# Attention's small results in PSUM banks of their own, the first batch's states turned ahead of the rest, and another order of the interleaved steps, in a block-recurrent attention and switch-routing kernel

## The chip, the cores and the metric

The kernel runs on one core of one Trainium2 chip, in one launch. The metric is device time in microseconds. All arithmetic is fp32 apart from a few counting matmuls in bf16.

## The reference

Eight batches, each with 8 heads, 512 tokens `x` and 32 states of width 64. Every token attends to the 32 states of its head and batch, and every state attends to the 512 tokens. The outcome is 8 x (512 + 32) = 4352 rows of 512 numbers, and each row is sent through one of eight experts, the one with the largest gate logit.

```python
scores = scale * np.matmul(x, state.transpose(0, 1, 3, 2))
a = np.exp(scores - scores.max(-1, keepdims=True)); a /= a.sum(-1, keepdims=True) + 1e-09
xread = np.matmul(a, state)
scores2 = scale * np.matmul(state, x.transpose(0, 1, 3, 2))
a2 = np.exp(scores2 - scores2.max(-1, keepdims=True)); a2 /= a2.sum(-1, keepdims=True) + 1e-09
sread = np.matmul(a2, x)
x = concatenate([xread, sread], axis=2).transpose(0, 2, 1, 3).reshape(B * S, H * D)
logits = x @ w_gate;  expert_idx = argmax(logits);  gate_w = softmax(logits)[expert_idx]
for e in range(E):
    xe = x[expert_idx == e]
    out[expert_idx == e] = gate_w * (np.maximum(xe @ w1[e], 0.0) @ w2[e])
```

## The kernel before

A token's row is a mix of the 32 states of its batch, so all 512 tokens of a batch lie close together and are taken to go to one expert, which `guess` works out from the states alone; a repair at the end handles batches where that fails. The matmul with `w1` is then done on the states (`states_w1`, giving `G`), not on the tokens. From batch 1 on, `lists` sorts the 1024 hidden units by a bound: units that are positive for every token (up to 512 of them, `CAPP`) need no relu and are folded into one matrix `M`; units of unknown sign (up to 192) are computed as they are. The kept units' columns of `G` are scattered to a table in DRAM (`g_dram`), loaded back in order (`gp`), and the matching rows of `w2` gathered (`w2c`). Batch 0 runs through `in_full` without that.

**The program's order is written out by hand.** Every engine keeps the order in which the code issues. The main line is `in_full` for batch 0 and `batch(b)` for batches 1 to 7; it calls `insert()` 16 times in batch 0 and 13 times in every later batch. I call these calls slots 0, 1, 2, ... In `batch(b)`: slot 0 follows the transposes `pgu`; slots 1 to 4 come after every second pair of matmuls into `pm`; slots 5 and 6 after the two `phu` groups; slots 7, 8 and 9 inside and after the first pair of `py` banks; slots 10, 11 and 12 inside and after the second. In a slot a plan (L763 and L765) advances generators by one step, one letter each:

- **A**, attention. `back(b)` has four steps: the transposes of `a2` with their copies `a2T`; the state sums `pw` and gate logits `pl`, with the loads of `x` for batch b+2; the norm bound `pq`; the expert count. Beside them run `front(b+1)`'s five: two halves of the transposes of `x`, the scores, the exponentials, the norm.
- **S**, `lists(b)` for a later batch: two steps for `G` (with the load of the next `w1`), four of transposes `pgt` and copies to `gt`, one of marks, one of ranks (`rank`) with eight scatters by GpSimd. The ninth step calls `fetch(b)`: three loads `gp` and six gathers `w2c`, all on GpSimd's queue.
- **M**, `mask(b+1)`, on VectorE.
- **R**, the 256 state rows, which go to experts one by one. When four batches are attended, `sort_states(t)` (five steps) puts 128 of them in groups of 32 by expert and scatters them to `ss_dram`; `rounds` then loads 128 rows (`xg`) and multiplies them by their experts' weights: two halves of `w1` (`pgh`), transposes (`pth`), and `w2` (`pgy`, in two halves of four pieces). There are three rounds, two for t = 0 and one for t = 1. A round takes 16 pieces of 1 MB, each four 256 KB loads on SyncE's queue into a ring of four buffers (`s`); after each group of four pieces is used, `fetch(4)` issues the next four, which wait for the buffers.

PSUM has 8 banks. Four belong to the tile `pa`: its half `pc` holds the scores, the other half (L95, `pa[:, :, 1, :]`) the small results of `guess` and `back`. The other four are handed out in turn by `bank()` (L98) for everything else. Order in the head: the states are loaded in one go (`stn`), all turned (`turn_states(0)`), all batches' experts guessed, the weights of batch 0 requested, then `turn_states(1)` and `front(0)`.

Of the kernel before, what the change touches and what calls it, by code (L numbers as in the profile page):

```python
# [20 lines left out]
def kernel(  # L21
# [39 lines left out]
    DM = H * D  # L61
# [33 lines left out]
    pa = ps_a.tile([128, 4, 2, 256], FP32, name="pa")  # L95
    pc = pa[:, :, 0, :]

    def bank(shape=(128, 512), name="p"):  # L98
# [3 lines left out]
    stn = att.tile([128, 16, D], FP32, tag="a2", name="stn")  # L102
    sp.dma_start(out=stn[:].rearrange("p j d -> p (j d)"),
                 in_=state.rearrange("b h (u j) d -> (b h u) (j d)", u=2))
# [8 lines left out]
    load_x(0, sp)  # L113
    wg = const.tile([128, NDC, E], FP32)
    act.dma_start(out=wg[:], in_=moe_w_gate.rearrange("(c p) e -> p c e", p=128))
    load_x(1, act)
# [32 lines left out]
    blank = att.tile([128, XW], I32, tag="a2T", name="blank")  # L149
# [10 lines left out]
    aTs, stT = {}, const.tile([128, B, H, 2, NS], FP32, name="stT")  # L160
# [9 lines left out]
    srow = const.tile([128, NT, XW], FP32)  # L170
    more = const.tile([128, NT], FP32)


    std = [sst.tile([128, 16, 2, D], FP32, tag="s", bufs=RING, name="std") for _ in range(2)]
    for i in range(2):
        dve.tensor_copy(out=std[0][:, :, i], in_=stn[:])
    for i in range(2):
        act.copy(std[1][:, :, i, 0:32], stn[:, :, 32:64])
        act.copy(std[1][:, :, i, 32:64], stn[:, :, 0:32])
# [10 lines left out]
    def turn_states(v):  # L190
        to = stT[:].rearrange("p b h v (u j) -> p v j (b h) u", u=2)
        for k in range(4):
            pt = pa[:, k].rearrange("p a (j r) -> p (a j) r", j=2) if v == 0 else bank((128, 4, 128), "pst")[:]
            for i in range(4):
                j = 4 * k + i
                pe.transpose(pt[:, i, :], std[v][:, j].rearrange("p i d -> p (i d)"), ident[:])
            evict(to[:, v, ts(k, 4)], pt.rearrange("p j (m u) -> p j m u", u=2))

    def guess():
        for b in range(B):  # L200
            for q in range(4):
                for g in range(2):
                    pe.matmul(pa[ts(q, 32), 2 + g, 1, ts(b, E)], lhsT=stT[ts(g, 64), b, 2 * q + g, 0, :],
                              rhs=wg[ts(g, 64), q, :], start=True, stop=True, skip_group_check=True)
        act.copy(gst[:, :, :, 0:E].rearrange("p b g e -> p g b e"),
                 pa[:, 2:4, 1, 0:B * E].rearrange("p g (b e) -> p g b e", b=B))
        pr = pa[:, 0, 1, 0:B * E].rearrange("p (b e) -> p b e", b=B)
        for g in range(2):
            pe.matmul(pr, lhsT=ones_f[:], rhs=gst[:, :, g, 0:E], start=(g == 0), stop=(g == 1),
                      skip_group_check=True)  # L210
        mx = att.tile([128, B, 1], FP32, name="g_mx")
        dve.tensor_reduce(mx[:, :, 0], pr, AX.X, ALU.max)
        cc = att.tile([128, B, E], FP32, name="g_cc")
        dve.tensor_tensor(cc[:], pr, mx[:].to_broadcast([128, B, E]), ALU.is_ge)
        dve.tensor_tensor(cc[:], cc[:], io8[:].unsqueeze(1).to_broadcast([128, B, E]), ALU.mult)
        dve.tensor_reduce(eb[:], cc[:], AX.X, ALU.max)
        dve.tensor_scalar(e_at[:], eb[:], float(F), None, ALU.mult)
# [19 lines left out]
    def scores(xt, st):  # L237
        for g in range(2):
            for u in range(2):
                for q in range(4):  # L240
                    for i in range(4):
                        pe.matmul(pa[ts(q, 32), i, 0, ts(g, 128)], lhsT=st[ts(i, 32), 2 * q + g, u ^ (i % 2), :],
                                  rhs=xt[ts(i, 32), 2 * q + g, :, u, :],
                                  start=(u == 0), stop=(u == 1), skip_group_check=True)
# [24 lines left out]
    def front(b):  # L269
# [5 lines left out]
        sx = scores(xt, stT[:, b])  # L275
# [16 lines left out]
    def back(b):  # L292
        sx, a2, s2 = soft.pop(b)
        aTs[b] = turn_read(sx)
        if b > 0:
            sq = att.tile([128, 2, S], BF16, tag="sq", name="sq")
            act.activation(sq[:], tokens_of(aTs[b]), AF.Square, bias=off[:, 0:1])
        a2T = att.tile([128, 2, NC, 128], FP32, tag="a2T", name="a2T")
        for g in range(2):
            for c in range(NC):  # L300
                pe.transpose(pa[:, 2 * g + c // 2, 1, ts(c % 2, 128)], a2[:, g, c, :], ident[:])
            act.copy(a2T[:, g].rearrange("p (k c) r -> p k (c r)", k=2), pa[:, ts(g, 2), 1, :])
# [3 lines left out]
        pw = pa[:, 0, 1, 0:128].rearrange("p (g d) -> p g d", g=2)  # L306
# [12 lines left out]
        pl = pa[:, 1, 1, 0:128]  # L319
# [5 lines left out]
        dve.transpose(lg[:].rearrange("p c e -> p (c e)"), pl)  # L325
# [11 lines left out]
        pr = pa[:, 2, 1, 128:128 + E]  # L337
        for c in range(NC):
            pe.matmul(pr, lhsT=ones_b[:], rhs=oh[:, NC * b + c, :], start=(c == 0), stop=(c == NC - 1),
                      skip_group_check=True)  # L340
        dve.tensor_copy(out=cnt[:, b], in_=pr)
# [40 lines left out]
    def states_w1(w1t, st, G, k):  # L382
        pg = [bank(name="pG") for _ in range(2)]
        for q in range(4):
            for g in range(2):
                pe.matmul(pg[g][ts(q, 32), :], lhsT=st[ts(g, 64), 2 * q + g, 0, :],
                          rhs=w1t[ts(g, 64), q, ts(k, 512)], start=True, stop=True, skip_group_check=True)
        for g in range(2):
            evict(G[g][:, ts(k, 512)], pg[g][:])
# [48 lines left out]
    def lists(b):  # L438
# [3 lines left out]
        for k in range(2):  # L442
            states_w1(w1t, stT[:, b], G, k)
# [51 lines left out]
    def fetch(b):  # L495
# [3 lines left out]
        for u in range(2):  # L499
            gp.dma_start(out=t[ts(u, 64), NP + 1], in_=g_dram[b % 2][ds(CAPP + 128, 64)])  # L500
        rows = moe_w2.rearrange("e f d -> (e f) d")
        w2cs[b] = [wpool.tile([128, DM], FP32, tag="w2c", bufs=W2B, name="w2c") for _ in range(NP + NU)]
        for j in range(NP + NU):
            gp.indirect_dma_start(
                out=w2cs[b][j][:], out_offset=None, in_=rows,
                in_offset=bass.IndirectOffsetOnAxis(ap=t[:, j, GW - 1:GW].bitcast(I32), axis=0),
# [14 lines left out]
    def batch(b, insert):  # L521
        t, w2c, a = gps.pop(b), w2cs.pop(b), aTs.pop(b)
# [8 lines left out]
        for g in range(2):  # L531
# [5 lines left out]
            act.copy(M[:, g, :], pm[:])  # L537
        hu = [ffn.tile([128, S], FP32, tag="hu", bufs=NU, name="hu") for _ in range(NU)]
# [25 lines left out]
    def sort_states(t):  # L564
        sp.dma_start(out=srow[:, t, 0:DM], in_=st_dram[ts(t, 128)])
# [4 lines left out]
        for c in range(NDC):  # L570
            pe.transpose(pt[:, c, :], srow[:, t, ts(c, 128)], ident[:])
# [3 lines left out]
        for c in range(NDC):  # L575
# [21 lines left out]
        dve.tensor_copy(out=srow[:, t, DM:DM + 1], in_=gw[:, NX + t])  # L597
        dve.tensor_copy(out=srow[:, t, DM + 1:DM + 2].bitcast(I32), in_=tok_s[:, t:t + 1])
        gp.indirect_dma_start(
            out=ss_dram[t][:], out_offset=bass.IndirectOffsetOnAxis(ap=slot_i[:, 0:1], axis=0),  # L600
            in_=srow[:, t, :].bitcast(I32), in_offset=None, bounds_check=NG * 32 - 1, oob_is_err=False)
# [10 lines left out]
    def rounds(t, r0, r1):  # L612
# [4 lines left out]
        def round_in(r):  # L617
            xgs[r] = sst.tile([128, XW], FP32, tag="xg", bufs=1, name="xg")
            sp.dma_start(out=xgs[r][:].bitcast(I32), in_=ss_dram[t][ts(r, 128)])
# [25 lines left out]
        for r in range(r0, r1):  # L645
# [22 lines left out]
            py = bank(name="pgy")  # L668
            for f in range(NFC):
                four(py, hT[:, ts(f, 128)], r, 2, f, 0, f == 0, f == NFC - 1)  # L670
                if f == 3:
                    fetch(4)
                    yield
            y = ffn.tile([128, DM], FP32, tag="y", bufs=3, name="ys")
            dve.tensor_scalar(y[:], py[:], xg[:, DM:DM + 1], None, ALU.mult)
# [7 lines left out]
    turn_states(0)  # L683
    guess()
    load_w1(0, expert_of(eb, 0))
    w2x = load_w2(expert_of(eb, 0))
    off = const.tile([128, 1], FP32)
    gp.memset(off[:], -1.0 / NS)
    U128 = const.tile([128, 128], BF16)
    dve.tensor_scalar(U128[:], colf[:], iota_p[:, 0:1], None, ALU.is_gt)  # L690
    turn_states(1)
    for _ in front(0):
        pass
# [4 lines left out]
    def late_constants():  # L698
        tmp = const.tile([128, 1], FP32)
# [9 lines left out]
        dve.scalar_tensor_tensor(slot_u[:, 1:2], iota_p[:], 128.0, tmp[:], ALU.add, ALU.add)  # L709

    attended = [0]

    def attention():
        for b in range(B):
            for _ in run(back(b), *([front(b + 1)] if b + 1 < B else [])):
                yield
# [3 lines left out]
    listed = [0]  # L720

    def listing():
        for b in range(1, B):
            for i, _ in enumerate(lists(b)):
                while i == 5 and bounded[0] < b:
                    yield
                yield
            fetch(b)
            listed[0] = b
            yield  # L730

    def masking():
        for b in range(1, B):
            while listed[0] < b:
                next(todo["S"])
# [10 lines left out]
    todo = {"A": attention(), "S": listing(), "R": tokens(), "M": masking()}  # L746
# [12 lines left out]
    for k in range(2):  # L759
        states_w1(w1t, stT[:, 0], G, k)  # L760
    load_w1(1, expert_of(eb, 1))
    late_constants()
    in_full(G, aTs[0], w2x, store_batch(0), inserts("A,A,AS,AS,AS,AS,AS,AS,S,S,S,A,AS,AS,AS,ASM"))  # L763
    for b in range(1, B):
        batch(b, inserts("SA,SA,SA,SA,SA,SR,SR,SR,SR,AR,RA,RA,RM"))  # L765
    for k in "ASMR":
# [30 lines left out]
    with tc.If(number(rest_i[0:1, 0:1], B * E + NT * NG) > 0):  # L797
# [4 lines left out]
        with tc.If(number(n_i[0:1, 0:1], B * E) > 0):  # L802
# [8 lines left out]
            with tc.For_i(0, n_pairs, 1):  # L811
# [23 lines left out]
                st_x = att.tile([128, 1, H, 2, NS], FP32, tag="sq", name="st_x")  # L835
                dve.tensor_copy(out=st_x[:], in_=stT[:, ds(bb, 1)])
# [9 lines left out]
                sx = scores(xt, st_x[:, 0])  # L846
# [21 lines left out]
                for k in range(2):  # L868
                    states_w1(w1s["x"], st_x[:, 0], G, k)
# [32 lines left out]
```

## Time and profile before

| | us |
|---|---|
| four runs: median (lowest to highest) | 571.96 (570.4 to 573.04) |
| the profiled execution | 573.04 |
| its span, first to last instruction | 571.2 |
| busy: TensorE / VectorE / GpSimd / ScalarE | 449.9 / 200.8 / 130.4 / 125.5 |

TensorE's stages, by the first transposes `pgu` of each batch (for batch 0 by its first matmul `pG`):

| stage | from, to (us) | length | TensorE busy | DMA share |
|---|---|---|---|---|
| head | 0 to 37.2 | 37.2 | 15.72 | 0.84 |
| batch 0 | 37.2 to 117.2 | 80.0 | 69.58 | 0.48 |
| batch 1 | 117.2 to 172.7 | 55.5 | 45.23 | 0.39 |
| batch 2 | 172.7 to 235.2 | 62.5 | 44.95 | 0.48 |
| batch 3 | 235.2 to 357.5 | 122.3 | 100.86 | 0.79 |
| batch 4 | 357.5 to 426.6 | 69.1 | 56.34 | 0.57 |
| batch 5 | 426.6 to 469.8 | 43.2 | 30.70 | 0.42 |
| batch 6 | 469.8 to 541.5 | 71.7 | 62.85 | 0.84 |
| batch 7 and the end | 541.5 to 571.2 | 29.7 | 23.62 | 0.15 |

Lines of the timeline give the start, the duration, the engine (PE is TensorE's matmul, PEld its weight load, DVE VectorE, ACT ScalarE, POOL GpSimd, SP SyncE, a q its queue), the operation, output<-inputs and the count; in brackets stand the engine's idle time before it and what ended that. A busy TensorE is not one at its peak: matmuls are pipelined and a matmul that waits inside a group stretches the group.

### The profile page before, as it was taken

What the parts mean: (1) busy time and instruction counts of PE and PEld (TensorE: products, weight loads), DVE (VectorE), ACT (ScalarE), POOL (GpSimd) and SP (SyncE); (2) the same over time, 40 slices, a digit from 0 to 9 for tenths busy, and PEclk for the clock granted to TensorE, in tenths of its full rate; (3) what the DMA queues carried; (4) which work ended last, traced back from release to release, by engine and by line L of the source; (5) the groups of instructions that cost most, each with busy time, mean ns of one, the idle gap of its engine ahead of it and who ended that gap; (6) DMA issues with size and microseconds to landing.
All of it is one profiled execution on the core that took longest, in us unless ns stands there. A gap on an engine that the chain in (4) does not pass through costs nothing. (4 is left out here: it accounts for less than half of the span.)

```text
span 571.2 us, 8799 instructions
## 1 busy us (share of the span) xinstructions
PE 449.9 (79%) x3277; PEld 185.9 (33%) x3284; DVE 200.8 (35%) x579; ACT 125.5 (22%) x217; POOL 130.4 (23%) x163
## 2 busy tenths in 40 slices
PE   3658799877975699397898589876899829788995
PEld 2523453442432334342131141432143414121241
DVE  2586573385447336454010202821043502000300
ACT  3132413224204114313010021330023212000021
POOL 6200006404330442005230000053204523340000
PEclk9859899977978869688999979988999969999998
DMA  8946422920750437944999878719721478999312
GB/s 270 282 149 219 148 93 75 346 78 33 254 187 37 123 111 277 287 142 134 350 388 317 267 220 292 267 41 341 267 82 48 143 223 277 300 365 315 113 38 76
DMA packets 58112, 113.89 MB, mean 199 GB/s; under 512 B 7511, under 2 KB 17058, under 8 KB 58064
## 3 DMA queue, kind: packets, MB, share of 16 engines
q1 hardware_dynamic: 42720, 78.92, 41.4%
q0 software_dynamic: 9152, 24.89, 13.1%
q10 hardware_dynamic: 6192, 9.46, 4.6%
q8 instruction: 28, 0.46, 0.3%
q14 instruction: 20, 0.16, 0.1%
HBM read 95.99 MB, written 20.62 MB: 204 GB/s over the span
## 5 line engine op out<-in xcount | busy, mean ns | idle before, releaser
L51 POOL DMA_INDIRECT g_dram<-gt,to x56 | 55.1, 983 | 255.3 <-DVE to L51 180.4
L51 PE MATMUL pgy<-s,shT 128*32 128x512 f32 x192 | 59.5, 621 | 14.0 <-DMA s<-in_moe_w_dram 12.9
L51 PE MATMUL pgh<-s,sxT 128*32 128x512 f32 x192 | 51.0, 644 | 11.9 <-DMA s<-in_moe_w_dram 8.1
L51 PE MATMUL pm<-w2c,gp 128*128 128x512 f32 x112 | 59.5, 671 | 0.2 <-ACT y L51 0.2
L51 PE MATMUL py<-M,aT 128*128 128x512 f32 x112 | 57.2, 635 | 0.9 <-DVE G L51 0.9
L51 POOL DMA_INDIRECT w2c<-in_moe_w_dram,gp x42 | 42.9, 1022 | 52.6 <-DMA gp<-g_dram 41.2
L51 DVE BATCH_NORM_STATS2 bn<-gt 128x6 f32<-128x256 f32 x56 | 21.0, 416 | 94.1 <-ACT gt L51 94.1
L51 PE MATMUL py<-w2c,hu 128*128 128x512 f32 (+1 forms) x112 | 44.0, 617 | 0.0
L51 ACT ACTIVATE y<-py,gw 128x512 f32<-128x512 f32 x32 | 22.0, 686 | 90.9 <-PE py L51 71.6
L51 PE MATMUL pa<-xt,stT 32*32 32x128 f32 x1024 | 25.1, 314 | 12.1 <-issue 7.9
L51 PE MATMUL pa<-ident,a 128*128 128x128 f32 x64 | 13.9, 356 | 25.5 <-ACT a2T L51 18.6
L51 PE MATMUL phu<-aT,Gu 128*128 128x512 f32 x56 | 32.0, 704 | 0.2 <-issue 0.2
L51 ACT COPY gt<-pgt 128x512 f32<-128x512 f32 x28 | 16.4, 587 | 67.1 <-PE pgt L51 64.5
L51 PEld LDWEIGHTS pgy<-s,shT 128*32 128x32 f32 x192 | 10.8, 110 | 60.8 <-DMA s<-in_moe_w_dram 51.9
L51 PEld LDWEIGHTS py<-M,aT 128*128 128x128 f32 x112 | 20.8, 202 | 29.0 <-issue 26.0
L51 PE MATMUL py<-w2x,hx 128*128 128x512 f32 x64 | 28.7, 598 | 0.0
L51 PEld LDWEIGHTS pm<-w2c,gp 128*128 128x128 f32 x112 | 21.7, 210 | 20.7 <-issue 19.8
L51 DVE TENSOR_SCALAR ys<-pgy,xg 128x512 f32<-128x512 f32 x3 | 2.3, 751 | 70.3 <-PE pgy L51 70.3
L51 PEld LDWEIGHTS pgh<-s,sxT 128*32 128x32 f32 x192 | 9.4, 114 | 52.1 <-DMA s<-in_moe_w_dram 35.9
L51 DVE COPY G<-pG 128x512 f32<-128x512 f32 x16 | 11.0, 690 | 42.8 <-PE pG L51 28.0
L51 PEld LDWEIGHTS pa<-xt,stT 32*32 32x32 f32 x1024 | 15.3, 111 | 22.1 <-issue 14.4
L51 PEld LDWEIGHTS py<-w2c,hu 128*128 128x128 f32 (+1 forms) x112 | 14.9, 187 | 19.8 <-issue 19.7
(181 smaller groups left out, 508.5 us busy)
## 6 DMA issues: line engine op xcount, KB each, us to landing
s<-in_moe_w_dram SPq DMA_DIRECT2D x192, 256.0 KB
w1t<-in_moe_w_dram SPq DMA_DIRECT2D x8, 2048.0 KB
out_dram<-y ACTq DMA_DIRECT2D x32, 256.0 KB
x_nat<-in_x_dram SPq DMA_DIRECT2D x14, 512.0 KB
gp<-g_dram POOLq DMA_DIRECT2D x7, 642.5 KB
w2x<-in_moe_w_dram SPq DMA_DIRECT2D x2, 1024.0 KB
ss_dram<-blank POOLq DMA_DIRECT2D x6, 257.0 KB
g_dram<-blank POOLq DMA_DIRECT2D x10, 128.5 KB
```

The source lines that it names most:

```text
L51: ins = getattr(self.engine, name)(*args, **kw)
```

## The change

PSUM: `pa` is now four whole banks for the scores alone, and every small result takes a bank from the ring of four. In `back`, the square `sq` moves from ahead of the copies `a2T` to behind the state sums.

```diff
-    pa = ps_a.tile([128, 4, 2, 256], FP32, name="pa")
-    pc = pa[:, :, 0, :]
+    pa = ps_a.tile([128, 4, 512], FP32, name="pa")
+    pc = pa[:, :, 0:256]
...
         for g in range(2):
+            pt = bank((128, NC, 128), "pa2")
             for c in range(NC):
-                pe.transpose(pa[:, 2 * g + c // 2, 1, ts(c % 2, 128)], a2[:, g, c, :], ident[:])
-            act.copy(a2T[:, g].rearrange("p (k c) r -> p k (c r)", k=2), pa[:, ts(g, 2), 1, :])
+                pe.transpose(pt[:, c, :], a2[:, g, c, :], ident[:])
+            act.copy(a2T[:, g], pt[:])
...
-        pw = pa[:, 0, 1, 0:128].rearrange("p (g d) -> p g d", g=2)
+        pw = bank((128, 2, D), "pw")
...
-        pl = pa[:, 1, 1, 0:128]
+        if b > 0:
+            sq = att.tile([128, 2, S], BF16, tag="sq", name="sq")
+            act.activation(sq[:], tokens_of(aTs[b]), AF.Square, bias=off[:, 0:1])
+        pl = bank((128, 128), "pl")
...
-        pr = pa[:, 2, 1, 128:128 + E]
+        pr = bank((128, E), "pcnt")
```

Head: the states come in three loads, batch 0 first, in pieces of 256 B where one load of 4 KB pieces stood; batch 0's are turned and its expert guessed alone, the other batches' states are turned between the steps of `front(0)`, and their experts guessed in the first step of a new generator **K**, between batch 0's `pG` and `ph`.

```diff
+    def load_states(i, b0, b1):
+        sp.dma_start(out=std[i][:, :, 0:D], in_=state[b0:b1].rearrange("b (g h) n d -> (h n) (b g) d", g=2))
...
-    load_x(0, sp)
+    load_states(0, 0, 1)
...
-    load_x(1, act)
+    load_x(0, sp)
+    load_states(1, 1, B - 1)
+    load_states(2, B - 1, B)
+    load_x(1, sp)
...
-    turn_states(0)
-    guess()
+    f0 = front(0)
...
+    turn_states(0, 2, 0, act.copy)
+    turn_states(0, 2, 1, copy_dve)
+    for t in std[1:]:
+        act.copy(t[:, :, 64:128], t[:, :, 0:64])
+        act.copy(t[:, :, 128:160], t[:, :, 0:32])
+    next(f0)
+    guess(0, 1)
     load_w1(0, expert_of(eb, 0))
...
+    for k0, k1 in ((5, 9), (9, 13), (13, 16)):
+        for v in range(2):
+            turn_states(k0, k1, v, act.copy)
...
     def late_constants():
+        guess(1, B)
```

Rounds: the rows `xg` get two buffers and are loaded by GpSimd's queue; `w2` is multiplied in two groups, each with a bank of its own, that VectorE adds.

```diff
-            xgs[r] = sst.tile([128, XW], FP32, tag="xg", bufs=1, name="xg")
-            sp.dma_start(out=xgs[r][:].bitcast(I32), in_=ss_dram[t][ts(r, 128)])
+            xgs[r] = sst.tile([128, XW], FP32, tag="xg", bufs=2, name="xg")
+            gp.dma_start(out=xgs[r][:].bitcast(I32), in_=ss_dram[t][ts(r, 128)])
...
+            for u in range(2):
+                py = bank(name="pgy")
+                for f in range(4 * u, 4 * u + 4):
+                    four(py, hT[:, ts(f, 128)], r, 2, f, 0, f == 4 * u, f == 4 * u + 3)
+                if u == 0:
+                    dve.tensor_scalar(y[:], py[:], xg[:, DM:DM + 1], None, ALU.mult)
...
+            dve.scalar_tensor_tensor(y[:], py[:], xg[:, DM:DM + 1], y[:], ALU.mult, ALU.add)
```

Order: the fetch leaves **S** for a generator **F**, which issues the loads `gp` with three gathers, and in another step the other three; attention may run up to three batches past the main line.

```diff
     def attention():
         for b in range(B):
+            while done[0] < b - 3:
+                yield
...
+    def fetching():
+        for b in range(1, B):
+            while listed[0] < b or done[0] < b - 1:
+                yield
             fetch(b)
-            listed[0] = b
+            fetched[0] = b
+            yield
+            while summed[0] < b - 1:
+                yield
+            gather(b, NP + NU - 3)
             yield
...
-    in_full(G, aTs[0], w2x, store_batch(0), inserts("A,A,AS,AS,AS,AS,AS,AS,S,S,S,A,AS,AS,AS,ASM"))
+    in_full(G, aTs[0], w2x, store_batch(0), inserts("A,A,AK,AS,AS,AS,AS,AS,AS,SA,SA,FA,FSA,SA,SA,SAM"))
     for b in range(1, B):
-        batch(b, inserts("SA,SA,SA,SA,SA,SR,SR,SR,SR,AR,RA,RA,RM"))
+        done[0] = b
+        batch(b, inserts("FS,SA,SR,SA,SR,FS,SA,SR,A,R,A,AR,MR"))
```

Followed through by the generators' own counts, the plans place the long steps so:

| step | before: batch, slot | after: batch, slot |
|---|---|---|
| ranks and scatters for batch 2 / 7 | 1, 3 / 6, 3 | 1, 2 / 6, 2 |
| first copy to `gt` for batch 3 | 1, 7 | 1, 6 |
| scores of batches 4 / 5 / 6 / 7 | 1, 10 / 2, 4 / 3, 2 / 4, 0 | 1, 8 / 2, 8 / 3, 8 / 4, 8 |
| attention of batch 7 done | 4, 11 | 5, 10 |
| t = 0: rows scattered, first `ptx` | 2, 9 and 2, 12 | 2, 11 and 3, 4 |
| round 0: `pgh`, `pgh`, `pgy`, `pgy` | 3, slots 5, 6, 8, 9 | 3, slots 7, 9, 12; 4, slot 2 |
| round 1: the same | 3, slots 11, 12; 4, slots 6, 7 | 4, slots 7, 9, 12; 5, slot 2 |
| t = 1: rows scattered, `ptx` | 5, 9 and 5, 12 | 6, 7 and 6, 12 |
| its round | 6, slots 5, 6, 8, 9 | 7, slots 2, 4, 9, 11 |

## The prediction

> **What bounds the kernel now.** I read the page's slices first. TensorE (PE) is busy 79% of the span, but unevenly, and where it is not, the DMA row is either full or nearly empty:
>
> ```profile
> PE   3658799877975699397898589876899829788995
> PEclk9859899977978869688999979988999969999998
> DMA  8946422920750437944999878719721478999312
> ```
>
> Each digit is a slice of 14.3 us. Counted from 0, slices 19 to 25 and 32 to 36 have full DMA: the rounds. Slices 9, 12, 26, 29 and 30 have almost none. So the loads come in bursts. The list of waits then says what PE stands for:
>
> ```profile
> PEld pgy L51 <- DMA s<-in_moe_w_dram: 51.9, 60, 4.7
> PEld pgh L51 <- DMA s<-in_moe_w_dram: 35.9, 40, 2.6
> PE ptx L51 <- DMA xg<-ss_dram: 21.7, 3, 10.6
> PE pa L51 <- ACT a2T L51: 18.6, 8, 5.1
> ACT sq L51 <- DVE s L51: 15.6, 5, 5.0
> ```
>
> (Totals in us, times, longest.) Last PE's timeline, here one `a2T` wait, one long weight group, and the longest `xg` wait:
>
> ```profile
> 133.19 0.86 PE L51 MATMUL pa<-ident,a 128*128 128x128 f32 x4
> 136.59 0.66 PE L51 MATMUL pa<-ident,a 128*128 128x128 f32 x4 [2.54 <-ACT a2T L51]
> 137.08 3.58 PE L51 MATMUL phu<-aT,Gu 128*128 128x512 f32 x4
> ...
> 306.29 5.03 PE L51 MATMUL pgy<-s,shT 128*32 128x512 f32 x18
> 312.78 1.66 PE L51 MATMUL pgy<-s,shT 128*32 128x512 f32 x4 [1.46 <-DMA s<-in_moe_w_dram]
> ...
> 468.93 1.09 PE L51 MATMUL ptx<-ident,xg 128*128 128x128 f32 x4 [10.59 <-DMA xg<-ss_dram]
> ```
>
> Two things beyond the gaps. After an `a2T` wait PE is slow for a while: these four `phu` matmuls take 3.58 us, the next four 1.98 (the windows show the granted clock at 0.50 from 138 to 140 us). And a group of 32 round matmuls that has its pieces takes 3.64 us, while the same group from 306.29 on ends at 320.60, after 14.31; only part of that shows as gaps.
>
> **The change, part by part.** The sum is made against the profiled execution, 573.04 us (span 571.2, 1.84 around it), which lies 1.08 above the median of 571.96.
>
> *Banks for the small results: -26.7, and +12 back.* The second four transposes of `a2` write other columns than the first copy reads, and still wait for it. With `pa2` in banks of its own they need not, and the copy itself no longer stands behind `sq`, which waited up to 5.0 us for VectorE. All eight waits go: 18.6. The slow stretch behind six of them goes too: against 1.98 for four matmuls, 3.29, 3.58, 2.80, 3.62, 3.15 and 3.54, together 8.1. But eight more allocations a batch now go through four banks, two of which `py` holds across slots 7 and 8. No row shows that. Bounds: nothing, or the whole 26.7 again. A bank is free again after a copy of 0.59 us behind one or two others on ScalarE, about 1.5 us, once a batch in eight batches: 12.
>
> The Trainium skill, "TensorE: Matmul & The Clock Gate" (Part 1, the two states), has the clock halved only after an idle window of about 3.4 us. By that rule only the waits of 5.12 and 3.41 us would have a slow stretch behind them, and that gain would be 2.5 instead of 8.1, the sum 5.6 higher. The row has the slow stretch behind 2.54 us, and I go by the row.
>
> *A wait moved forward: +10.* `gt` has one buffer. The next list's first copy into it waits for the last list's eight scatters. In batch 1 ranks were ready at 129.71 and that copy's transposes came at 147.22, 17.5 us later, just after the scatters (eight at 1.28 us, 10.2, from 134.53). Now ranks come at slot 2 and the copy at slot 6. PE's work between is two `pm` pairs (3.76), two `phu` groups (3.6), `G` (2.05) and the transposes (0.9), 10.3 us; the scatters and their landing need some 14 (1.5 for VectorE, 10.2, 2). ScalarE and VectorE stand at that copy, and behind them relu, `pw` and `pl`; PE follows when the four banks are full. I take 3.3 us in batches 1, 2 and 5, where no weight load hides it: 10. Bounds: 0 and 5 x 7.
>
> *`xg`: -14.7.* The three waits are 6.08, 4.99 and 10.59. For t = 0, `ptx` moves from three slots behind the scatter to some six: gone. Round 1's load waited for the single buffer: gone. For t = 1 GpSimd decides: 8 scatters, `gp` and its landing took 19.5 us from the ranks (433.2) to the first gather (452.73); then come three gathers (4.0) instead of six (8.0), the row scatter's landing (5.35) and the load (2.68), 31.7 us in all. PE has 20.9 us of slots and 2 of sorting to fill that: 8.8 remain. 21.7 - 8.8 = 12.9, and some 1.8 of slow clock behind the first two (transposes of 1.06 to 1.09 us a group where warm ones take 0.45 to 0.60). The loads now wait on GpSimd's queue, with the scatters and gathers behind them; those need their data ten slots later. Bounds: -21.7 and 0.
>
> *Rounds spread: -43.9.* The 12 groups of four pieces now last, from first to last matmul with the waits before them, 5.34, 14.28, 11.57, 14.31, 3.64, 14.20, 3.64, 20.46 for t = 0 and 3.64, 18.70, 9.64, 13.39 for t = 1: 132.8, against 12 x 3.64 = 43.7. So 89.1 us are lost to loads. A burst brings four pieces in 14.3 us (4.2 MB, 293 GB/s beside other traffic). After the change the main line's work stands between the groups: in a round of t = 0, 6.1 us before the second, 8.4 before the third, 4.9 before the fourth, 16 or more before the next round. With 3.64 for the group itself, 4.5, 2.3 and 5.8 us are left of 14.3: 12.6, twice. In batch 7 it is 3.8, 11.4 and 5.6 us: 6.9, 0 and 5.1. Together 37.2; with 8 for the 2 MB of `w1` that each of two rounds finds in the queue, 45.2. Gain 43.9. What hides the loads is batches 3 and 4; without that cover they cost 89.1 again. The split of `pgy` adds three operations of VectorE of 0.75 us off the path.
>
> *Head: -2.5.* `pG` begins at 37.24. Today experts are known at 19.42 and the scores begin at 24.72, behind VectorE's state copies. In the new order ScalarE's copies of the other states stand ahead of the guess, so it waits for their load: `x` and the states (1.6 MB) share the queues with the blanks, some 13 us; four copies (1.8), the guess as before (3), weights requested at 18, scores at 18.3, 6.4 earlier. Six state copies then stand on ScalarE ahead of `a2T`, 1.2 us: `pG` at 32. The other seven batches' guess (1.6 of its 1.82 us, and 1.1 for the sums) now stands between `pG` and `ph`: 2.7. The request of `w1` for batch 1, at 41.03 on SyncE's queue today, comes behind that guess too, some 4 us later in its stage; its first use, 10.95 us after the request, moves back by a slot and the guess, about 5: covered, and otherwise up to 4 lost. `x` of batch 1 moves from ScalarE's queue to the end of SyncE's and is due only after batch 0's scores. Bounds: -10 (weights requested at 10) and +5 (states as late as today's scores).
>
> "DMA: Bandwidth & Descriptors" of the skill (Specifications) wants pieces of 512 B or more; below, the engine reads, modifies and writes. These are 2048 pieces of 256 B. No run here shows such pieces; by the rule the gain in the head is nothing, the sum 2.5 higher.
>
> *Costed at nothing:* scores issued beside GpSimd's indirect transfers came out at 8.7 and 10.6 us instead of 1.9; now slot 8 may meet the gathers again: between -15 and +15. F's split moves three gathers behind R's transfers on GpSimd's queue; their rows are due four slots later.
>
> 573.0 - 26.7 + 12 + 10 - 14.7 - 43.9 - 2.5 = 507.2, less 1.1 for the median: **506 us**.
>
> **Rivals.** *The loads gain nothing (0.22).* Attention isn't ahead for long: 17 steps instead of 14 in batch 0, then 6 a batch instead of 8, so batch 7's ends in batch 5 and the last round falls into batch 7, where nothing follows. If a group still waits as long as now, the 43.9 fall away: 550. For it: the ring is four pieces as before, and the next four are requested only when four are used. Against: batches 4 and 5 had a DMA share of 0.57 and 0.42.
>
> *Banks take their gain back (0.12).* If PE waits for a bank as long as it did for `a2T`, 26.7 stands instead of 12, and `gt` costs 20 instead of 10: 506 + 14.7 + 10 = 531. For it: VectorE reads `pw`, `pl` and counts in its own order. Against: ScalarE is 22% busy.
>
> *Slower (0.08).* One mechanism: at slot 6 PE fills the four banks at once and stands until the scatter has landed, in batches 1 to 5. Its price is today's whole distance, 17.5 us a batch, so 506 - 10 + 88 = 584. It decides from 15 us a batch on. Against: the 10.3 us of work between need none of these banks for long.
>
> **The numbers.** The forecast has 0.55; no change in effect 0.03. Adding the favourable ends of banks (12), `gt` (10) and half of head and `xg` (8) gives 476; the first rival with some of its own spread 558. Range 472 to 558. About half a percent is what a measurement of this kernel can tell from none. Faster by over 0.5%: 0.55 + 0.22 + 0.12 = 0.89; within: 0.03; slower: 0.08.
>
> **What would show it.** In the new profile: `pG` near 32; no wait for `a2T`; one `xg` wait, near 9, at the end of batch 6; round groups summing to 89 rather than 133; idle DMA gone from batch 4; new waits of PE for VectorE or ScalarE around slots 6 to 8. Batches 3 and 4, 191 us now, should take about 137, and batch 7 over 50 instead of 30. The forecast is wrong if round groups still come to 120 or more, or if TensorE's idle time behind ScalarE and VectorE grows by over 25.

## The result, and the profile after

The changed kernel takes **534.47 us** (median of 22 runs, 514.09 to 546.65) beside 572.44 for the kernel before (32 runs, 568.54 to 576.15). The ratio is 0.9037, with a 95% interval of 0.8988 to 0.9086; it counts undisturbed runs only, which of the changed kernel are the two at 514.09 and 520.53, so it lies below the ratio of the medians, 0.934. The profiled execution took 528.26 us (span 526.4), 21 more than the sum of 507.2 that was made for it.

First the page's slices of the changed kernel (PE, granted clock, DMA; 13.2 us each):

```profile
PE   1588996894977797788889969999979795089992
PEclk9989997777986899979979998999989899589997
DMA  9976611733176106886999999998551118929791
```

Counted from 0, DMA is full in slices 19 to 26, and PE is at 9 in all but two of slices 20 to 28, where it went down to 5 in the rounds before. Slices 30 to 32, the end of batch 5 and the first half of batch 6, are without loads, since nothing is to be fetched between the last piece of t = 0 and the first of t = 1. Batch 4, from which the forecast had the idle DMA gone, has a DMA share of 0.97 now (0.57 before). The deepest hole left for PE is slice 34 (0), with DMA at 9 in it. The granted clock is the same on the mean, 0.903 (0.904 before). The list of waits (totals in us, times, longest) says what PE stands for now:

```profile
PE ptx L51 <- DMA xg<-ss_dram: 24.8, 2, 20.6
PE pgu L51 <- issue: 12.5, 2, 6.9
PE prg L51 <- ACT gst L51: 10.5, 2, 10.2
PE pa L51 <- issue: 10.1, 24, 0.8
PE pw L51 <- issue: 9.1, 14, 2.5
PE pgu L51 <- DVE gp L51: 7.5, 2, 3.8
PE pw L51 <- ACT G L51: 4.9, 2, 3.2
...
PEld pgh L51 <- DMA s<-in_moe_w_dram: 23.1, 35, 2.0
...
PEld pgy L51 <- DMA s<-in_moe_w_dram: 19.8, 35, 1.4
```

The waits for pieces fell from 51.9 and 35.9 to 19.8 and 23.1, and `a2T` is not in the list at all. The group of `pgy` that lasted 14.31 us from 306.29 on in the kernel before lasts 9.84 now:

```profile
295.94 8.56 PE L51 MATMUL pgy<-s,shT 128*32 128x512 f32 x30
304.73 1.05 PE L51 MATMUL pgy<-s,shT 128*32 128x512 f32 x2 [0.24 <-issue]
```

The wait of `prg` is batch 0's first guess, in the head. Three things are larger or new: the wait for `xg` in batch 6 is 20.6 in one piece, the first transposes of a batch (`pgu`) wait 20.0 us in all, and `pa` and `pw` have waits put down to "issue", in which the engine waits for nothing that the profile shows. The timeline of PE shows the first two, and the eight transposes of `a2` in one go where there had been two fours with a wait between:

```profile
126.44 1.12 PE L51 MATMUL pgu<-ident,gp 128*128 128x128 f32 x4 [6.88 <-issue]
...
134.96 1.04 PE L51 MATMUL pa<-ident,a 128*128 128x128 f32 x8
...
462.11 1.08 PE L51 MATMUL ptx<-ident,xg 128*128 128x128 f32 x4 [20.60 <-DMA xg<-ss_dram]
```

The third shows in the scores of batch 4, which run in slot 8 of batch 1: 128 small matmuls that take 1.90 us elsewhere. Here is PE's timeline, and below it GpSimd's in the same stretch:

```profile
156.59 1.35 PE L51 MATMUL pa<-xt,stT 32*32 32x128 f32 x80
158.15 0.39 PE L51 MATMUL pa<-xt,stT 32*32 32x128 f32 x3 [0.21 <-issue]
158.88 0.42 PE L51 MATMUL pa<-xt,stT 32*32 32x128 f32 x4 [0.35 <-issue]
...
166.22 0.74 PE L51 MATMUL pa<-xt,stT 32*32 32x128 f32 x15 [0.34 <-issue]
...
157.56 1.07 POOL L51 DMA_INDIRECT w2c<-in_moe_w_dram,gp  x1 [8.66 <-DMA gp<-g_dram]
158.93 1.04 POOL L51 DMA_INDIRECT w2c<-in_moe_w_dram,gp  x1 [0.31 <-issue]
```

Eighty matmuls go through in 1.35 us. GpSimd issues its first indirect gather at 157.56, and from 158.15 to 166.22, a microsecond past the end of the sixth gather at 165.19, only 33 matmuls come, in handfuls of three to five. The group lasts 10.38 us, until 166.97. I call this a crawl.

| Length from batch to batch (first `pgu` to the next), us | before | after |
|---|---|---|
| head (to the first `pG`) | 37.2 | 31.5 |
| batch 0 | 80.0 | 95.0 |
| batches 1, 2 | 55.5, 62.4 | 55.1, 44.4 |
| batches 3, 4 | 122.3, 69.2 | 65.5, 69.6 |
| batches 5, 6 | 43.2, 71.7 | 53.0, 48.9 |
| batch 7 and the end | 29.7 | 63.4 |

### The profile page after: what moved, and what is told of

The parts are those of the page before. It is cut to its first block, busy times and chain, and to the rows that moved or that the text cites. A ratio compares the mean times of both kernels' runs of the same rounds, so it can differ in the third digit from the quotient of the medians.

```text
span 526.4 us, 8828 instructions
## 1 busy us (share of the span) xinstructions
PE 418.6 (80%) x3281; PEld 181.4 (34%) x3288; DVE 199.5 (38%) x582; ACT 124.1 (24%) x226; POOL 132.2 (25%) x166
## 3 DMA queue, kind: packets, MB, share of 16 engines
q1 hardware_dynamic: 45296, 79.18, 44.2%
## 4 chain that ended last, share of the span: by engine, by line
PE 58%; DMA 16%; issue 9%; DVE 6%; ACT 4%; SPq 3%; POOL 1%; another core or an unknown queue 1%; ACTq 1%; POOLq 0%; DVEq 0%
PE py L51 19%; DMA s<-in_moe_w_dram 9%; PE pm L51 8%; PE pa L51 5%; PE phu L51 5%; PE pgy L51 5%; PE pgh L51 3%; PE pG L51 3%; SPq L51 3%; DMA w1t<-in_moe_w_dram 2%; DMA xg<-ss_dram 2%; DMA std<-in_state_dram 2%; PE pw L51 2%; PE pgt L51 2%; ACT y L51 2%
## 5 line engine op out<-in xcount | busy, mean ns | idle before, releaser
L51 POOL DMA_INDIRECT g_dram<-gt,to x56 | 55.1, 984 | 231.2 <-DVE to L51 186.5
L51 PE MATMUL pgh<-s,sxT 128*32 128x512 f32 x192 | 40.4, 607 | 2.8 <-DMA s<-in_moe_w_dram 2.7
L51 PE MATMUL pa<-xt,stT 32*32 32x128 f32 x1024 | 30.6, 320 | 13.4 <-issue 10.1
L51 PE MATMUL pgy<-s,shT 128*32 128x512 f32 x192 | 40.2, 600 | 1.1 <-DMA s<-in_moe_w_dram 0.5
L51 PE MATMUL py<-w2x,hx 128*128 128x512 f32 x64 | 31.9, 650 | 0.0
L51 PE MATMUL phu<-aT,Gu 128*128 128x512 f32 x56 | 28.4, 636 | 0.8 <-issue 0.8
L51 PEld LDWEIGHTS pa<-xt,stT 32*32 32x32 f32 x1024 | 16.7, 112 | 26.9 <-issue 23.1
L51 DVE STREAM_TRANSPOSE sx<-pa 128x256 f32<-128x256 f32 x32 | 11.5, 418 | 34.0 <-PE pa L51 34.0
L51 PE MATMUL pw<-x_nat,a2T 128*32 128x64 f32 x512 | 12.8, 224 | 13.9 <-issue 9.1
L51 PE MATMUL ptx<-ident,xg 128*128 128x128 f32 x12 | 2.8, 380 | 24.8 <-DMA xg<-ss_dram 24.8
L51 PE MATMUL pgu<-ident,gp 128*128 128x128 f32 x28 | 6.6, 367 | 20.0 <-issue 12.5
L51 DVE COPY shT<-pth 128x512 f32<-128x512 f32 x3 | 2.1, 686 | 50.3 <-PE pth L51 50.3
## 6 DMA issues: line engine op xcount, KB each, us to landing
g_dram<-blank POOLq DMA_DIRECT2D x10, 128.5 KB
```

Source lines behind the costliest of these rows:

```text
L51: ins = getattr(self.engine, name)(*args, **kw)
```

## The experiments

There are twelve runs, of eleven kernels (run seven repeats run six), in four sets. Each set has its own runs of the kernel before (median 573.46, 561.0, 560.6 and 573.77 us), so kernels of different sets are compared by their ratios to it. The changed kernel's own runs spread so widely that a difference from it depends on which number is taken, its median (534.47) or its ratio (0.9037); both are given.

**One: plain loads in place of the gathers**

```
-            gp.indirect_dma_start(out=w2cs[b][j][:], ..., in_=rows, in_offset=...gps[b][:, j, GW - 1:GW]...)
+            gp.tensor_copy(out=seen[:], in_=gps[b][:, j, GW - 1:GW])
+            gp.dma_start(out=w2cs[b][j][:], in_=rows[ds((6 * b + j) * 128, 128)])
```

> The six gathers of each batch become plain loads of the same bytes (128 rows of 2 KB of w2) from fixed places on GpSimd's queue, each behind a small GpSimd copy that reads the list it read before, so that they start no earlier. The rows of w2 that stand in M and in the unclear units' sum are therefore others than the lists name; everything else is computed as before. Theory: it is the issue of indirect transfers on GpSimd that makes TensorE's small matmuls crawl. Then the scores that took 9.19, 10.38 and 10.32 us in batches 0, 1 and 3 come to 1.9 each, pw of batch 5 from 4.49 to 1.1, and pw of batch 0 beside the scatters, which stay indirect, remains at 5 to 9: about 28 us less, near 507. Rival: what slows them is the traffic of the transfers, or any transfer issued on GpSimd; then these groups stay at 8 to 10 us and the time stays near 534.

It took 499.75 us (498.05 to 502.74), ratio 0.8756 (0.8706 to 0.8807). The scores of batch 0, PE first, then GpSimd's issues beside them:

```profile
103.31 1.90 PE L51 MATMUL pa<-xt,stT 32*32 32x128 f32 x128
...
103.06 0.54 POOL L51 DMA_DIRECT2D w2c<-in_moe_w_dram  x1
...
103.71 0.54 POOL L51 DMA_DIRECT2D w2c<-in_moe_w_dram  x1
```

The same bytes from the same queue at the same place, and the 128 matmuls take 1.90 instead of 9.19 us. Those of batch 3 (1.91, beside three loads) and `pw` of batch 5 (1.10, beside three) are normal too; those of batch 1 met no load this time. `pw` of batch 0, beside the scatters that stayed indirect, took 8.08. So it is something in the indirect form and not the traffic, which during the scores of batch 0 was higher here (363 GB/s, 203 there). What in that form does it (scattered rows, the list of indices, the longer issue) was not taken apart. The plain issues are also shorter, 0.54 against 1.0 us, and the batches after them had less to wait for, so not all of the time gained is the crawl's.

**Two: `xg` on SyncE's queue again**

```
-            gp.dma_start(out=xgs[r][:].bitcast(I32), in_=ss_dram[t][ts(r, 128)])
+            sp.dma_start(out=xgs[r][:].bitcast(I32), in_=ss_dram[t][ts(r, 128)])
```

> The load of a round's states (xg) goes back to SyncE's queue, with its two buffers kept. Theory: in batch 6 the sixteen piece loads, 4 MB, no longer pass ahead of the row scatter and of xg, because SyncE's queue stands at xg until the scatter has landed; the scatter lands in some 5.4 us instead of 10.5, xg in 2.7 instead of 5.6, so the wait of 20.6 us falls to 12 or less, and the first group of pieces after it waits longer in exchange, by up to 8: the time falls by 3 to 10, to 524 to 531. Rival: the scatter was late because of GpSimd's own queue (gathers ahead of it), not because of the pieces; then the wait stays at 18 to 21 and the pieces come later on top: 534 to 545.

It took 509.61 us (507.60 to 510.81), ratio 0.8913 (0.8861 to 0.8966): 25 below the changed kernel's median, far more than expected, but 7 by the ratios, which is what was expected. The wait in batch 6 fell from 20.60 to 13.74, not to 12: the scatter landed in 4.26 us, but the load still took 5.03. Batch 6 went from 48.9 to 42.6. But the larger part of what lies between the two profiles, 13.5 us, lies in batch 1 (55.1 to 41.6), where there is no round and no `xg` yet. Counted from the batch's first `pgu`, both traces agree to 0.02 us for the first 17 us; then `pw` begins 0.86 us later in the changed kernel (after a wait of 3.24, 2.39 here), the four `py` matmuls behind it take 3.19 instead of 1.98, and the scores start 30.1 instead of 27.6 us into the batch. The gathers start at 31.1 and 31.6. PE's scores in the `xg` run, and its first gather below:

```profile
155.18 1.90 PE L51 MATMUL pa<-xt,stT 32*32 32x128 f32 x128
...
159.12 1.07 POOL L51 DMA_INDIRECT w2c<-in_moe_w_dram,gp  x1 [9.14 <-DMA gp<-g_dram]
```

Here the scores are through before the gathers begin, there they are caught by them. So most of the 20 us between the two profiles is not the edit's: a delay of 2.5 us decides over 8.5 more (10.38 less 1.90). Such a chance may also be why the changed kernel's runs lie 33 us apart and those of this one 3; that was not tested.

**Three: the small results back in the score banks**

```
+        if b > 0:
+            sq = att.tile([128, 2, S], BF16, tag="sq", name="sq")
+            act.activation(sq[:], tokens_of(aTs[b]), AF.Square, bias=off[:, 0:1])
...
-            pt = bank((128, NC, 128), "pa2")
...
-        pw = bank((128, 2, D), "pw")
+        pw = pa[:, 0, 256:384].rearrange("p (g d) -> p g d", g=2)
...
```

> The small results of the attention (turned a2, pw, pl, counts) go back into the free halves of the four score banks, and the squares go back ahead of the copies on ScalarE; all else of the change stays. Theory: the four transposes of the second half wait again for the first half's copy, 2 to 5 us in each of seven batches and more slow TensorE behind it (before: 18.6 of waits and 8.1 behind them), while the new waits of pw (7.4 in all) go: 534 + 27 - 7 = 554, range 545 to 560. Rival: the order of the work has changed enough that the wait for a2T falls where TensorE would stand anyway; then the sum of these waits stays below 8 and the time below 540.

548.0 us (544.1 to 560.59), ratio 0.9564 (0.9503 to 0.9625): 14 above the changed kernel's median, 30 by the ratios. In the profiled execution, the one at 560.59, waits for `a2T` are back (11.9), and `pl` waits for VectorE's reading of `pw` (11.7), which now lies in the same tile. The traces differ in which small groups met the gathers, so the part was run again without that (run ten).

**Four: the rounds' steps late**

```
-"FS,SA,SR,SA,SR,FS,SA,SR,A,R,A,AR,MR"
+"FS,SA,S,SA,S,FSR,SAR,SR,AR,R,AR,AR,MR"
```

> Only the R steps move: eight a batch in its last eight slots, as before the change, instead of six spread over slots 2 to 12; attention stays ahead, everything else stays. Theory: spreading is what hides the pieces; the eight groups of t = 0 fall into two bursts again and take from first to last matmul about 14 us wherever four pieces were used just before, so the twelve groups sum to 115 to 135 instead of 84: 534 + 35 to 45, about 570. Rival: what hid them is that attention runs ahead and leaves the DMA queues freer from batch 4 on, not the slots; then the groups sum to less than 100 and the time stays below 548.

568.3 us (565.11 to 572.55), ratio 0.9929 (0.9891 to 0.9968): 34 above the changed kernel's median, 51 by the ratios. Nearly all of the change's gain is gone by this one line. The waits of PE:

```profile
PE ptx L51 <- DMA xg<-ss_dram: 32.3, 3, 22.2
PE pgh L51 <- DMA s<-in_moe_w_dram: 15.1, 14, 7.9
PE pgy L51 <- DMA s<-in_moe_w_dram: 11.8, 9, 3.3
```

The last two stand against 2.7 and 0.5 in the changed kernel. The twelve groups last 117.2 us from first to last matmul instead of 84.1. With the waits for pieces before the first matmul, as the prediction counted its 132.8, they come to 128.5 (the changed kernel has none, so 84.1 stays). Five of the six groups whose predecessor had just used four pieces last 13.8 to 17.8 again, and batch 3 takes 112.1 instead of 65.5. The steps of attention stand in the same slots as in the changed kernel, so it is the slots of the rounds that hide the loads.

**Five: the gathers held until the scores are through** (from run two)

```
+            gp.tensor_copy(out=at[b][:, 0:1], in_=seen_of.pop())
+            gp.tensor_copy(out=at[b][:], in_=gps[b][:, :, GW - 1].bitcast(I32))
             gather(b, 3)
```

with `seen_of` the scores' maximum or the attention's result, and the F steps put behind the scores' slot.

> Kernel of the xg run, and on GpSimd a copy of a column that the scores' maximum (in the last batches: the attention result) has written stands ahead of the six gathers of each batch, so that none is issued before the scores are through; their index column is copied once more, so that they depend on it. Nothing is left out, nothing made direct. Theory (issue of indirect transfers makes small matmuls crawl): no scores take over 2.8 us any more, pw of batch 5 comes to 1.1; pw of batch 0, beside the scatters, stays at about 8. Against 509.6 that takes 6.9 + 8.0 + 5.9 + 3.3 = 24 away: about 486, range 480 to 496. Rival: the gathers' rows are then late, and TensorE waits for w2c or the mask instead of crawling, in most batches by 3 us or more: 500 to 515.

496.35 us, ratio 0.8822 (0.8768 to 0.8876). No scores and no `pw` crawl any more. That holds for `pw` of batch 0 too, which took 1.10 us at 87.00 in the midst of the scatters (issued from 83.39 to 93.40), where the theory had it at about 8; why it escaped is not explained. The end of the crawl should have brought 24 us; by the ratios it brought 5. Batches 0, 5 and 6 are 16, 8 and 8 us shorter than in run two, but batches 1 and 2 are 6.5 and 4.7 longer, batch 4 is 3.9 and batch 7 6.2. `pgu` waits as long as in run two (20.4 and 20.0); new are the waits of the lists' transposes for `gt`, one in each of batches 1 to 3:

```profile
PE pgu L51 <- DVE gp L51: 14.8, 3, 6.9
PE pgt L51 <- ACT gt L51: 9.8, 3, 3.9
```

And the twelve groups of the rounds, which came to 80.3 us in run two, come to 103.5: with less time between the groups, it seems, more of the loads shows. The theory was right on the crawl of the scores, and its rival on the time.

**Six and seven: all kept apart, the mask sooner**

```
-"S,SA,SR,SA,SR,FS,SA,SR,A,FR,A,AR,MR"
+"S,SA,SR,SA,SR,FS,SA,SR,A,FR,FMA,AR,SR"
```

and batch 0's last slots from `SA,SA,A,SA,SAF,SA,SASFM` to `S,SA,SAF,A,AS,AS,AFFMSSS`; batch 1 gets a plan of its own, `S,S,SAA,SA,S,FS,SA,S,A,F,FMA,A,S`.

> As the held gathers, and two moves of slots. In batch 0 the attention of batch 2 comes one slot later (pw in slot 13, scores in 14, norm in batch 1 behind the rank), and the norm of slot 9 comes behind the rank, so that pw stands behind the scatters and not beside them. The mask of the next batch's list comes in slot 10, ahead of exp and norm on VectorE, instead of behind them in slot 12. Theory: pw of batch 0 comes from 8 to 1.1 us, and the waits of the first transposes of a batch for the mask (20.0 us in all) fall below 6: another 7 + 14 us less than the held gathers alone, about 466, range 458 to 478. Rival: the mask waits only stand for the time that the gathers and the list need anyway, so that the wait moves to the rows (pm waits for w2c) or to the list's copy: less than 6 us gained against the held gathers.

484.5 us, ratio 0.8629 (0.8559 to 0.8698). Run once more in the third set:

> The kernel of all moves once more, on the chip of the next three, so that they can be compared with it there. The theory expects 0.863 of the kernel before, as there; no rival.

480.2 us, ratio 0.8573 (0.8524 to 0.8622). The `pgu` waits are down to 4.0, from 20.4 in run five, and 11 to 14 us were gained on it (0.019 and 0.025 of 573). That is less than the 21 expected, since `pw` was well already in run five. The move of the mask and the new slots of batches 0 and 1 were not tried apart. VectorE's timeline in the changed kernel shows what stood ahead of the mask at the end of batch 0:

```profile
121.32 1.20 DVE L51 TENSOR_REDUCE sm<-sx 128x32 f32<-128x1024 f32 x1
...
123.16 1.22 DVE L51 TENSOR_TENSOR sx<-sx,sm 128x1024 f32<-128x1024 f32 x1
124.30 1.40 DVE L51 BATCH_NORM_STATS2 bn<-gt 128x6 f32<-128x256 f32 x4
125.62 0.21 DVE L51 TENSOR_SCALAR mk<-slot_p,nn 128x4 f32<-128x4 f32 x1
...
125.99 1.67 DVE L51 TENSOR_SCALAR gp<-gp,mk 128x256 f32<-128x256 f32 x6
```

The norm of the next front and statistics of the following list, 4.3 us from 121.32 on, none of them needed for batch 1's first transposes, which need the mask; `pgu` follows at 126.44.

**Eight: the first guess ahead of the state copies** (from run six)

```
-    for t in std[1:]:
-        act.copy(t[:, :, 64:128], t[:, :, 0:64])
...
     w2x = load_w2(expert_of(eb, 0))
+    for t in std[1:]:
+        act.copy(t[:, :, 64:128], t[:, :, 0:64])
```

> All moves, and in the head ScalarE's copies of the other seven batches' states come behind the first guess instead of ahead of it. Theory (the prediction's: the guess waits for that load): batch 0's expert is known near 6 us instead of 15.6, w1 is requested by 8 to 9 instead of 16.3, and the first pG matmul comes at 27 to 29 instead of 32.2; 3 to 5 us less, and the 2 to 3 us more that the head was worth. Rival: pG waits for batch 0's own attention (turned a2, after scores and exp), so it stays at 31 to 32 and the time the same.

485.69 us, ratio 0.8664 (0.8595 to 0.8733): no gain on run seven (its batches are 1 to 2% longer almost throughout), and the reason is neither of the two. SyncE's queue and PE:

```profile
9.03 0.39 SPq L51 DMA_DIRECT2D w1t<-in_moe_w_dram  x1
...
19.55 1.15 PE L51 MATMUL pa<-ident,a 128*128 128x128 f32 x8
31.47 1.88 PE L51 MATMUL pG<-w1t,stT 64*32 64x512 f32 x9 [10.77 <-DMA w1t<-in_moe_w_dram]
```

`w1` is asked for at 9.03 instead of 16.34 and lands after 22.3 us instead of 15.7; the transposes of `a2` are through at 20.70. DMA moved 9.88 MB in the first 36 us without a pause (274 GB/s). That points to the bytes asked for ahead of `w1` as the head's limit; run eleven tests it.

**Nine: the lists two slots sooner** (from run six; the plan of batch 1, then that of the later batches)

```
-"S,S,SAA,SA,S,FS,SA,S,A,F,FMA,A,S" / "S,SA,SR,SA,SR,FS,SA,SR,A,FR,FMA,AR,SR"
+"A,SA,SA,S,S,F,SA,S,A,FS,FMSA,A,S" / "S,SA,SR,SA,R,F,SA,SR,A,FSR,FMSA,AR,SR"
```

> All moves, and from batch 1 on the list of the next batch comes two slots sooner (rank in slot 0 or 1 instead of 2), so scatters, list load and gathers too. Theory: with the crawl gone the chain on GpSimd (eight scatters 10.7 us, their landing, the list's load and landing some 12, six gathers 7.7) sets the length of batches 1, 2 and 5, 45.1, 47.2 and 41.5 us; two slots sooner, 38 to 42 each: 8 to 18 us less than the kernel of all moves, a ratio of 0.832 to 0.85. Rival: TensorE's own work or the scores that hold the gathers set it, so that less than 4 us are gained.

467.7 us (467.31 to 471.46), ratio 0.8366 (0.8308 to 0.8425): 12.5 us less than run seven beside it. (Batch 0's last slot also advances the list by two more steps.) Batches 1 and 2 went from 44.2 and 47.2 to 41.6 and 41.0, and the waits of `pgt` for `gt`, that is for the scatters, from 11.1 to 1.5. That fits the theory that, with the crawl gone, those batches wait for GpSimd's chain of scatters, list load and gathers. In its place `rank` waits 12.3 us for VectorE's `marks`, and batch 3 became 4.6 longer.

**Ten: the banks back, with nothing else in the way** (run six and the edit of run three)

> All moves, but the small results of the attention back in the score banks' free halves and the squares ahead of the copies on ScalarE, as in the other run of this kind, now where no small matmuls crawl beside gathers. Theory: the banks part by itself is worth what it was forecast at, 26.7 less 12, so this is 11 to 19 us slower than the kernel of all moves, with waits for a2T of 10 or more. Rival: 14 us in the other run came from small matmuls that met the gathers by other timing; then 5 us or less.

494.0 us, ratio 0.8802 (0.8743 to 0.8861): 13.8 us above run seven, in the same set. Between the two profiles 8.9 us lie in batch 0.

```profile
PE pa L51 <- DVE xs L51: 15.4, 8, 5.9
PE pa L51 <- ACT a2T L51: 14.6, 8, 4.8
```

**Eleven: the head ordered by need** (from run nine): `load_x(1)` and `w2` behind `w1`, the guess first, the blanks behind batch 0's scores.

> The kernel with the sooner lists, and a head ordered by need: the first guess ahead of the copies of the other states; then w1 of batch 0, only then x of batch 1 and w2; and the 2.9 MB of blanks are written after batch 0's scores. Theory: the head is bound by the bytes that are requested ahead of w1 (9.9 MB at 274 GB/s up to 36 us in the run with the guess first), not by when it is requested; with some 4 MB up to and with w1, w1 lands before 21 us, pG begins at 22 to 24, where batch 0's own attention is through, instead of 33.1, and the time falls by 7 to 11 us, to a ratio of 0.817 to 0.825. Rival: what was moved back is late in batch 0 instead (x for its scores, w2 for py, w1 of batch 1): pG comes early, but batch 0 is longer by as much, and less than 3 us are left.

472.05 us beside 573.77, ratio 0.8201 (0.8118 to 0.8283). The first `pG`:

```profile
21.54 2.06 PE L51 MATMUL pG<-w1t,stT 64*32 64x512 f32 x32
```

11.5 us sooner than in run nine, without a wait. But batch 0 takes 81.3 instead of 72.3, and batch 1 begins 2.5 us sooner than there, 4.2 sooner than in run twelve. Theory and rival share it: the scores for batch 1 (7.67 us, 2.72 in run nine) waited 0.62 for the turned `x` and then stood 3.77 us in an issue gap, which is not explained. The time is 6.8 us less than run twelve, in the same set, which also loads `xg` on the other queue; by the ratios it is some 9 less than run nine, whose only difference is the head. It is the fastest version found, 18% below the kernel before.

**Twelve: `xg` on GpSimd's queue, nothing else in the way** (run nine with the changed kernel's queue)

> The kernel with the sooner lists, but the load of a round's states on GpSimd's queue, as in the changed kernel. Theory: on GpSimd's queue the load stands behind the gathers and, in batch 6, the sixteen piece loads pass ahead of it, so the wait of 2.2 us for xg comes to 8 or more, mostly in batch 6, and the kernel is 4 to 12 us slower. Rival: with lists and scatters sooner the row scatter is sooner too, and the queue makes no difference: within 2 us.

478.84 us, ratio 0.8369 (0.8306 to 0.8432), the same as run nine within some 5 us, as the two ran in different sets; so the lower end of the 4 to 12 expected is not ruled out. The wait did grow, from 2.2 to 10.5, the longest 8.0. But batch 6 took 34.6 instead of 28.4 and batch 7, up to its last matmul, 53.8 instead of 59.3: what PE waits longer for `xg`, it waits less for the pieces that land meanwhile.

## Why the prediction was right, and where it was not

The forecast was 506, the range 472 to 558; 534 lies inside, and "faster" held. The miss is 28 us by the median, 21 for the profiled execution and 11 by the ratio. The largest step, the rounds, holds in kind and in size; the next, the banks, holds in its net.

- *Rounds spread, -43.9.* Right. The groups came to 84.1 us (88.9 forecast), batches 3 and 4 to 135.1 (137), batch 7 to over 50; undone by itself, 34 us of the time come back (51 by the ratios). The rival with 0.22, "the loads gain nothing", falls with it.
- *Banks, -26.7 and +12 back.* All `a2T` waits went, and the net, 14.7, was measured as 13.8 in run ten. That the two lie so close is in part luck: the halves were not measured apart, the changed kernel's list shows no waits for banks that come near 12, and run ten has 30 us of waits back for 13.8 of the time. The slow stretch behind a wait was seen once more: four `py` take 3.19 us behind `pw`'s wait of 3.24, and 1.98 behind run two's of 2.39. The rival with 0.12 (531) falls, though its time came nearest: it needed 26.7 taken back and `gt` at 20.
- *A wait moved forward, +10.* Three waits of `pw`, 3.24, 2.52 and 1.61, in batches 1, 2 and 3, make 7.4. The rival on the slow side needed 15 us a batch and got at most 3.24 of it.
- *Head, -2.5.* `pG` at 31.46 (32 forecast). The reason was half right: the guess does wait for the other states' load (10.24 us), but that wait costs next to nothing, since with the same loads beside it `w1` landed at 31.3 to 32.1 whether it was asked for at 9.0, 16.3 or 18.9 us (runs eight, six and nine). The step's lower bound, -10 by an early request, was not to be had that way; it takes fewer bytes ahead. The states' pieces of 256 B did no harm that shows: batch 0's, asked for at 0.75 us, were being turned at 3.21.
- *`xg`, -14.7.* Wrong in what it said of the trace: 8.8 was to remain and 24.8 did, 20.6 in batch 6 and 4.2 in batch 4, where the wait was to be gone. What failed in batch 6 is that the landing of the row scatter and the load were taken over at 5.35 and 2.68 us. With `xg` off SyncE's queue, nothing holds that queue back, and sixteen piece loads (4 MB) go out from 434.98 to 454, eleven of them ahead of the scatter issued at 445.77. GpSimd's timeline:

```profile
445.77 1.03 POOL L51 DMA_INDIRECT ss_dram<-srow,t_si  x1 [0.30 <-issue]
...
456.32 0.60 POOL L51 DMA_DIRECT2D xg<-ss_dram  x1 [5.57 <-DMA ss_dram<-srow,t_si]
```

  The scatter took 10.5 and the load 5.7, together 8.2 of the 11.8 us too many there. Run two, with the queue held, had 4.3 and 5.0: the scatter became faster, the load hardly. Run twelve shows that such a wait is partly paid back by the pieces, so its 16 us too many are not 16 of the time.
- *Costed at nothing: scores beside indirect transfers, between -15 and +15.* This is the step that failed. In all, five groups crawled instead of three (8.24, 9.19, 10.38, 10.32 and 4.49, where 7.9 is normal for all five): 34.7 us lost against 17.5 before, +17, beyond the bound. The row was on the page with its two long groups; it was taken for an accident of the old order, and no place of the new order was checked for it. In batch 1 slot 8 is 30 us into the batch and the gathers come at 31.
- *Not forecast: the mask.* `pgu` waited 5.3 us in all before and waits 20.0 now. Attention running ahead puts the next front's norm and bn_stats of another list on VectorE right ahead of the mask. The text asked what is queued behind `gt` on ScalarE and VectorE, and did not ask what stands ahead of the mask. Moving it, with batch 0's slots, gave 11 to 14 us.

Crawl, mask and `xg` come to 48 us of waits too many, against 21 of time; the small favourable misses of rounds, `gt` and head take some 8 off, and the rest is probably overlap of the kind that runs five and twelve show, where a wait taken away came back as another. Their shares in the 21 were not measured apart.

## What to carry to other kernels

Work that is spread over slots hides its loads even when nothing is loaded sooner: one line of the plan was worth 34 us here, by the medians. But each step that moves must be placed in time against the other engines' issues, not only against what it depends on; where a group of many small matmuls can meet indirect transfers, keep them apart by a dependence rather than by luck of 2 us. And when a wait is removed, look for the chain that was as long: here it was first the mask on VectorE, then the lists on GpSimd, and in the head the bytes.

## What the runs showed of the hardware

While GpSimd issues indirect transfers, dense groups of small matmuls on TensorE can fall from 128 in 1.90 us (67 a us) to 3 to 6 a us: in the changed kernel 33 scores in 8.07 us in batch 1, 19 in 7.39 in batch 3, and 18 matmuls of `pw` in 2.99 in batch 5. Plain loads of the same bytes beside them did nothing of the kind in run one.

The crawl does not set in at once. Of batch 0's scores and the `pw` of batches 0 and 5, all begun 1.4 to 3.6 us after the first indirect issue beside them, the first 30, 43 and 43 matmuls still came at the usual pace. A group of 32 round matmuls at 327.49 of the changed kernel, beside gathers, took 3.64 us as always; but it is hardly longer than that head start, so it does not show that larger matmuls are safe. Nor does it look like one fixed limit on instructions: with its weight loads that group is 64 instructions in 3.64 us, 17.6 a us, while the crawling scores above come to 5 to 8. The runs don't show the cause. Not every issue catches a group: `pw`, 64 matmuls, beside scatter issues took 1.10 in runs five and six and 2.91 in run twelve.
